# A clock per half of the TensorE array in the scheduler of a fused attention and feed-forward kernel

## Chip, cores and metric

The kernel runs on one core of a Trainium2 chip. The metric is the device time of one execution in microseconds (us); the time that counts is the median of several executions. Profiles come from one further execution each.

## What is computed

`x` is 2048 x 512. A gate per row mixes an attention with 32 query heads, head size 16 and a single shared key and value head, and a feed-forward layer with SiLU:

```python
q = (x @ wq).reshape(B, S, 32, 16).transpose(0, 2, 1, 3)
k, v = x @ wk, x @ wv                          # 2048 x 16 each, shared by all heads
p = softmax(einsum("bhqd,bkd->bhqk", q, k) * 16 ** -0.5)
a = einsum("bhqk,bkd->bhqd", p, v).transpose(0, 2, 1, 3).reshape(B, S, 512) @ wo
b = silu(x @ w1) @ w2                          # w1: 512 x 1792, w2: 1792 x 512
g = sigmoid((x * gate_w).sum(-1, keepdims=True))
out = g * a + (1 - g) * b
```

The exponentials are 32 x 2048 x 2048 values, and they set the size of the problem: ScalarE takes them in 1024 instructions of 128 x 1024.

## The kernel before

**The work.** The attention is cut into 32 rounds: 4 chunks of 512 queries, 4 groups of 8 heads, 2 halves of a group. A round has 16 steps, one for each 128 keys, so there are 512 steps. A step has two parts; each part is one group of eight score products (`scores`, line 1174) into a two-bank PSUM tile `S` and one exponential (line 1180, ScalarE) from `S` to `P`. Then P V sums the step into `pv` (`sums`, line 1278). This is done in one of two ways. A *native* step multiplies the float32 `P` with `VF`. A *split* step takes the upper 16 bits of `P` as they lie (unit "U") and the rest `L` (unit "L"), which VectorE makes with one 128 x 2048 instruction (`low`, line 1199), and multiplies both with `VP`. A native step costs TensorE more, a split step costs VectorE one long instruction.

**The array.** All these products have few rows and columns, so TensorE is used as eight tiles of 64 rows x 32 columns: a lower half (partitions 0 to 63) and an upper half, with four column tiles each. A group of eight score products fills all eight tiles once; so do the eight products of a unit. `pv0` is summed on the lower half, `pv1` on the upper.

**The stream.** Beside the attention runs a stream of 512-column products, given out by the generator `outs()`: hidden blocks of the feed-forward layer (`ffn_h`, 12 products), its outputs (`ffn_o`, 12 or 6), later projections of queries (`q_block`, 12) and of the attention's results (`out_proj`, 12 or fewer). Each such output contracts over 128 rows: its products on the lower 64 rows and those on the upper 64 rows go into one PSUM bank `pm`. Before the change two outputs run in lockstep (`f_slot`, line 835 is the product): while output `cur` does its upper rows, the next output `new` does its lower rows, eight products at a time. When `cur` is done it is evicted (`leave`): by ScalarE's tanh (line 849) and VectorE (line 854), or by VectorE into `acc` (lines 807 and 809), and a new turn starts only when that eviction is over (`f_ready`).

**The order.** Nothing is scheduled by hand: `attention` runs a planner while the program is built. It keeps estimated clocks for TensorE (`pe`), ScalarE (`act`), VectorE (`dve`) and GpSimd (`pool`), a list of VectorE tasks with due times (`put`, `serve`), and in the loop `while p < n_s` decides what TensorE issues next: `sums`, `f_slot`, or the next `scores`, which may not come before the exponential two parts earlier has freed its `S`. The constants in capitals at the file's head are the planner's prices and thresholds: `SLOT` is one group, `PB` the number of `P` buffers, `HURRY` the number of steps behind from which P V goes first. Every engine takes its instructions in the order in which the planner emitted them; waits are semaphores.

**The end.** A round ends with `norm_a`: VectorE transposes `pv0` and `pv1` out of PSUM (lines 1103 and 1104), then GpSimd (in the last round VectorE) adds, rebuilds and normalizes; `turned` makes the 16-bit pairs `O` (lines 1135 and 1136) that `out_proj` needs. After the last scores, `attention` finishes the sums, then the outputs that still run, then all outputs that are left as whole 128-row products (`whole`, line 839), each evicted into `acc` and written out.

The rule that lets a turn of the stream start:

```python
if T_.evicted in tasks:
    return False
if max(T_.free, ahead[0].free if ahead else 0.0) > pe[0]:
    return False
```

## Time and profile before

| what | value |
|---|---|
| time, median of 3 (lowest, highest) | 1075.16 us (1074.93, 1075.76) |
| time of the profiled execution | 1073.23 us |
| its span, first to last instruction | 1071.4 us |
| granted TensorE clock, mean | 0.995 |
| busy: PE, ACT, DVE, POOL | 1023.1, 999.7, 916.6, 471.2 us |
| first exponential starts | 39.3 us |
| split steps (instructions of line 1199) | 245 |

How to read it: PE is TensorE, ACT ScalarE, DVE VectorE, POOL GpSimd. A row of a timeline has the start, the time until the last of the grouped instructions ends, engine, line, operation, out<-in, shape, count, and in brackets how long the engine sat idle before, and for whom. The recorded duration of a matmul holds its way through the array, so consecutive groups overlap in the records; what a group costs is the distance from its start to the next group's start. The clock column is the share of full speed that was granted to TensorE.

### The profile page before, as it was taken

How to read it: one execution, taken by the hardware profiler on the slowest of the kernel's cores; microseconds unless marked ns; L12 is line 12 of the kernel's file. 1: busy time of each engine (PE TensorE's matmuls, PEld its weight loads, DVE VectorE, ACT ScalarE, POOL GpSimd, SP SyncE). 2: the span in 40 equal slices, each digit the busy share in tenths (PEclk: the TensorE clock that was granted, in tenths of full speed). 3: DMA queues.
4: the chain of work that ended last, by engine and by line, in shares of the span. 5: the costliest groups of instructions: out<-in, count | busy, mean ns of one | idle time of the engine just before them, and what ended most of it. 6: DMA issues, size and time to landing. Idle time of an engine off the chain costs nothing.

```text
span 1071.4 us, 65086 instructions
## 1 busy us (share of the span) xinstructions
PE 1023.1 (95%) x30610; PEld 564.2 (53%) x30610; DVE 916.6 (86%) x838; ACT 999.7 (93%) x1121; POOL 471.2 (44%) x388
## 2 busy tenths in 40 slices
PE   8999999999999999999999999999999999999996
PEld 5465454455555545455555555555555555555452
DVE  6799989999999998788797878888889898889784
ACT  5799999999999999999999999999999999999980
POOL 1034345324352373634744335465475267374620
PEclk9999999999999999999999999999999999999998
DMA  5421211100000100000000010000000010000001
GB/s 199 135 61 49 70 41 54 51 12 22 8 18 31 31 22 11 12 19 16 12 22 11 12 60 12 19 7 22 12 11 11 12 47 8 12 11 12 4 5 42
DMA packets 23079, 32.90 MB, mean 31 GB/s; under 512 B 5137, under 2 KB 13074, under 8 KB 22802
## 3 DMA queue, kind: packets, MB, share of 16 engines
q1 hardware_dynamic: 22050, 27.54, 8.4%
q8 instruction: 241, 3.95, 1.6%
q0 software_dynamic: 320, 1.05, 0.3%
q14 instruction: 36, 0.29, 0.1%
q10 hardware_dynamic: 432, 0.07, 0.0%
HBM read 20.12 MB, written 8.52 MB: 27 GB/s over the span
## 4 chain that ended last, share of the span: by engine, by line
PE 38%; ACT 35%; DVE 13%; issue 8%; POOL 4%; DMA 1%; ACTq 0%; SPq 0%; DVEq 0%; POOLq 0%
ACT P L1180 33%; PE pm L835 13%; PE pv L1278 12%; PE S L1174 9%; DVE L L1199 7%; PE pm L839 2%; ACT e L849 2%; POOL T L1109 1%; POOL U L1111 1%; DVE e L854 1%; PE pt L316 1%; DVE acc L809 1%; POOL T L1112 1%; POOL H L856 0%; POOL U L1116 0%
## 5 line engine op out<-in xcount | busy, mean ns | idle before, releaser
L1180 ACT ACTIVATE P<-S 128x1024 f32<-128x1024 f32 x1024 | 959.6, 1079 | 24.4 <-PE S L1174 22.7
L1199 DVE TENSOR_TENSOR L<-P 128x2048 f16<-128x2048 f32 x245 | 606.8, 2491 | 35.8 <-ACT P L1180 35.2
L1174 PE MATMUL S<-qb,KT 50*32 50x512 f16 x8192 | 435.0, 380 | 13.5 <-ACT P L1180 11.0
L1174 PEld LDWEIGHTS <-KT 50*32 50x32 f16 x8192 | 191.6, 89 | 244.5 <-issue 161.1
L1278 PE MATMUL pv<-P,VF 64*32 64x512 f32 (+1 forms) x5360 | 298.2, 503 | 0.0
L835 PE MATMUL pm<-xs,w1s 64*32 64x512 f16 x5376 | 263.7, 375 | 2.3 <-DVE e L854 1.1
L835 PE MATMUL pm<-w2s,H 64*32 64x512 f16 x4896 | 249.2, 375 | 4.9 <-DVE acc L807 2.0
L1109 POOL TENSOR_TENSOR T<-T,U 128x512 f32<-128x512 f32 x31 | 83.8, 2704 | 275.4 <-DVE U L1104 275.4
L856 POOL CAST H<-e 128x512 f16<-128x512 f32 x56 | 57.7, 1030 | 205.9 <-DVE e L854 204.3
L835 PEld LDWEIGHTS <-w1s 64*32 64x32 f16 x5376 | 116.1, 92 | 53.3 <-issue 14.9
L835 PEld LDWEIGHTS <-H 64*32 64x32 f16 x4896 | 106.2, 92 | 46.5 <-issue 6.3
L1278 PEld LDWEIGHTS pv<-P,VF 64*32 64x32 f32 x5360 | 104.7, 106 | 37.4 <-issue 6.6
L857 POOL TENSOR_TENSOR H<-e,H 128x512 f16<-128x512 f32 x56 | 108.8, 1943 | 4.5
L1278 PE MATMUL pv<-P,VP 64*32 64x512 bf16 x1952 | 108.1, 388 | 1.2 <-DVE U L1104 0.6
L1278 PE MATMUL pv<-L,VP 64*32 64x512 f16 x1952 | 103.3, 375 | 3.1 <-DVE L L1199 2.8
L1278 PEld LDWEIGHTS <-VP 64*32 64x32 f16 x3904 | 67.8, 93 | 45.1 <-issue 20.9
L835 PE MATMUL pm<-xs,wqs 64*32 64x512 f16 x1152 | 83.9, 375 | 1.1 <-DVE e L854 1.0
L854 DVE SCALAR_TENSOR_TENSOR e<-e,pm 128x512 f32<-128x512 f32 x56 | 38.3, 683 | 43.2 <-ACT e L849 42.9
L835 PE MATMUL pm<-wo_s,O 64*32 64x512 f16 x1440 | 68.3, 382 | 3.2 <-DVE acc L809 1.8
L1116 POOL TENSOR_TENSOR U<-U 128x48 f32<-128x48 f32 (+1 forms) x62 | 57.4, 925 | 2.4
L809 DVE SCALAR_TENSOR_TENSOR acc<-pm,g,acc 128x512 f32<-128x512 f32 x48 | 35.7, 744 | 14.6 <-PE pm L839 8.0
L1111 POOL TENSOR_TENSOR U<-T,mu 128x96 f32<-128x96 f32 x31 | 45.5, 1468 | 2.4
(175 smaller groups left out, 623.6 us busy)
## 6 DMA issues: line engine op xcount, KB each, us to landing
qb<-qd SPq DMA_DIRECT2D x192, 32.0 KB
raw<-in_B_w_dram SPq DMA_DIRECT2D x22, 256.0 KB
xn<-in_A_x_dram SPq DMA_DIRECT2D x8, 512.0 KB
out_dram<-acc SPq DMA_DIRECT2D x16, 256.0 KB
qd<-qx SPq DMA_DIRECT2D x12, 256.0 KB
raw<-in_B_w_dram POOLq DMA_DIRECT2D x4, 256.0 KB, 3.1
raw<-in_A_wo_dram SPq DMA_DIRECT2D x4, 256.0 KB
qb<-sh SPq DMA_DIRECT2D x62, 2.0 KB
```

The lines of the kernel that those rows point to most:

```text
L809: nc.vector.scalar_tensor_tensor(a, po, gate[:, n:n + 1], a, op0=OP.mult, op1=OP.add)
L835: nc.tensor.matmul(self.bank[32 * m:32 * m + 32], l(i, rows, 32 * m), r(j, rows), start=first, stop=last)
L854: nc.vector.scalar_tensor_tensor(e, e, 1.0, ph, op0=OP.add, op1=OP.mult)
L856: nc.gpsimd.tensor_copy(H[:, 0], e)
L857: nc.gpsimd.tensor_tensor(H[:, 1], e, H[:, 0], op=OP.subtract)
L1109: eng.tensor_tensor(T, T, U, op=OP.add)
L1111: eng.tensor_tensor(z[:, :, 1:1 + DIGITS], T3[:, :, 17:17 + DIGITS], mu[:, :, 1:].to_broadcast([128, 16, DIGITS]), op=OP.mult)
L1116: eng.tensor_tensor(first, first, second, op=OP.add)
L1174: nc.tensor.matmul(sc[32 * m:32 * m + 32, f], KT[b:b + 50, k0:k0 + 32], qtile[i][b:b + 50, j], start=True, stop=True)
L1180: nc.scalar.activation(P[:, 2 * j:2 * j + 2], sc, AF.Exp, scale=scale_of(c, o))
L1199: nc.vector.tensor_tensor(L[s], P, upper(P), op=OP.subtract)
L1278: nc.tensor.matmul(pvs[i][h][32 * j:32 * j + 32, cols], a[r], b[r, j, cols], start=start, stop=rest == n)
```

## The change

The planner gets a clock for each half of the array, `half[0]` and `half[1]`, and `pe` only follows them.

- `sums(s, h)` emits the four products of one half; which steps are done, opened and closed is kept for each half, and the two halves of a step need not be neighbours. `norm_a` gets one PSUM task per half (one transpose each).
- The stream no longer runs in lockstep. Two banks `pm0` and `pm1` replace the pool of two; an output starts on whichever half is free, and its second part runs on the other half, once a later score group has waited for a semaphore that covers its first part (`synced`, `marks`) and `GUARD` has passed. `f_slot` emits four products of one output.
- `choose(h, ...)` decides for the half whose clock is behind; if it finds nothing, the other half is asked, then the next scores come.
- `low` of odd steps is made only if a step is at least `SPARE` = 1 ahead (before 0); `HURRY` goes from 4 to 5, so the stream goes ahead of P V for longer.
- After the last scores the remaining outputs run on both halves, and whole products are taken as soon as a bank is free, without first emptying VectorE's task list; the last attention outputs wait for their planned time instead of going first.

The core of the diff:

```diff
-SLOT, VSLOT, LOW, V_PART, BLOCK, ONE_LATE = 0.2165, 0.23, 2.37, 1.7, 3.65, 0.3
-LATER, HURRY, PIECE, PB, FIRST_LOW, LASTB, NEAR, FRESH, SPARE = 0.2, 4, 5.6, 5, 6, 4, 4, 8, 0
+SLOT, VSLOT, LOW, V_PART, BLOCK, ONE_LATE, GUARD = 0.2165, 0.23, 2.37, 1.7, 3.65, 0.2, 0.2
+LATER, HURRY, PIECE, PB, FIRST_LOW, LASTB, NEAR, FRESH, SPARE = 0.2, 5, 5.6, 5, 6, 4, 4, 8, 1
...
-        def issue(n, dur):
-            if sent[0] // 256 != (sent[0] + n) // 256:
-                pe[0] = crossed[0] = max(pe[0], crossed[0] + BLOCK)
-            sent[0] += n
-            pe[0] += dur
+        def issue(h, n, dur):
+            start = max(half[h], floor[0])
+            if sent[0] // 256 != (sent[0] + n) // 256:
+                start = crossed[0] = floor[0] = max(start, crossed[0] + BLOCK)
+            sent[0] += n
+            half[h] = pe[0] = start + dur
...
-        def f_slot():
-            i, cur, new = T_.i, T_.cur, T_.new
+        def f_slot(o, h):
             for m in range(4):
-                if new and i < new.n:
-                    new.product(i, lo, m, i == 0, False)
-                if cur and i >= T_.n - cur.n:
-                    cur.product(i - T_.n + cur.n, hi_, m, False, i == T_.n - 1)
-            issue(16, SLOT)
+                o.product(o.i, (lo, hi_)[h], m, o.i == 0 and not o.second, o.second and o.i == o.n - 1)
+            issue(h, 8, SLOT)
...
             for j in range(4):
-                for h, r in enumerate((lo, hi_)):
-                    nc.tensor.matmul(pvs[i][h][32 * j:32 * j + 32, cols], a[r], b[r, j, cols], start=start, stop=rest == n)
+                nc.tensor.matmul(pvs[i, h][32 * j:32 * j + 32, cols], a[r], b[r, j, cols], start=start, stop=rest == n)
...
+        def choose(h, now, room, behind):
+            n = sums_next(h, now, room, behind >= HURRY)
+            o = f_here(h, now) if room >= SLOT else None
+            if n is not None and last_of(n, h, room) and behind < LASTB and (not o or o.n - o.i < FRESH):
+                n = None
+            if n is not None and (behind >= HURRY or not o):
+                return lambda: sums(n, h, room)
+            if o:
+                return lambda: f_slot(o, h)
...
-                    urgent.extend((c, 0 if late else end, lambda t=t: out_proj(c, all_, t)) for t in range(4))
+                    urgent.extend((c, end, lambda t=t: out_proj(c, all_, t)) for t in range(4))
...
         while True:
-            while tasks:
-                do(min(tasks, key=lambda t: t[0]))
-            o = ahead.pop() if ahead else fetch()
-            if o is None:
+            now = pe[0] = max(half)
+            serve(now)
+            b = bank(now)
+            o = fetch(b) if b and not ended[0] else None
+            if o:
+                for n in range(o.n):
+                    o.whole(n, n == 0, n == o.n - 1)
+                    both(SLOT)
+                leave(o)
+            elif ended[0] and not tasks:
                 break
-            for n in range(o.n):
-                o.whole(n, n == 0, n == o.n - 1)
-            force(o.evict(o.bank))
+            else:
+                both(0.05)
```

What this moves is seen best at two places of the built programs. The first is TensorE's order at a native step right after a group of scores; the two names `pv_...` before are the sums of the lower and the upper half. Before:

```order
L1174 MATMUL S<-qb_81,KT 32x512
L1278 MATMUL pv_14627<-P,VF 32x512
L1278 MATMUL pv_14628<-P,VF 32x512
L1278 MATMUL pv_14627<-P,VF 32x512
L1278 MATMUL pv_14628<-P,VF 32x512
```

and at such a place now, where `pm_2837` is an output of the stream:

```order
L1174 MATMUL S<-qb_81,KT 32x512
L1290 MATMUL pv_2803<-P,VF 32x512 x4
L840 LDWEIGHTS wqs
L840 MATMUL pm_2837<-xs,wqs 32x512
L840 LDWEIGHTS wqs
L840 MATMUL pm_2837<-xs,wqs 32x512
```

The eight products of a native step alternated between the halves; now four products of one half stand together, and the other half's stream stands behind them.

The second place is VectorE's order from the last round's sums (line 1116 ends them) to the last output. `pm` is an output's bank; `g_65` marks an output of the feed-forward layer, `gg` one of the attention. Before:

```order
L1116 TENSOR_TENSOR T<-T,U 128x16
L809 SCALAR_TENSOR_TENSOR acc<-pm,g_65,acc 128x512
L1124 RECIPROCAL rr<-T 128x16
L1127 TENSOR_TENSOR C<-T,rr 128x16x16
L1133 STREAM_TRANSPOSE T<-C 128x512
L1135 CAST O<-T 128x512
L1136 TENSOR_TENSOR O<-T,O 128x512
L809 SCALAR_TENSOR_TENSOR acc<-pm,gg,acc 128x512 x4
L809 SCALAR_TENSOR_TENSOR acc<-pm,g_65,acc 128x512 x7
```

and now, up to the first of the four attention outputs:

```order
L814 SCALAR_TENSOR_TENSOR acc<-pm_32988,g_65,acc 128x512
L814 SCALAR_TENSOR_TENSOR acc<-pm_33021,g_65,acc 128x512
L1124 RECIPROCAL rr<-T 128x16
L1127 TENSOR_TENSOR C<-T,rr 128x16x16
L814 SCALAR_TENSOR_TENSOR acc<-pm_33392,g_65,acc 128x512
L1133 STREAM_TRANSPOSE T<-C 128x512
L1135 CAST O<-T 128x512
L1136 TENSOR_TENSOR O<-T,O 128x512
L814 SCALAR_TENSOR_TENSOR acc<-pm_33402,g_65,acc 128x512
L814 SCALAR_TENSOR_TENSOR acc<-pm_33415,g_65,acc 128x512
L814 SCALAR_TENSOR_TENSOR acc<-pm_33423,g_65,acc 128x512
L814 SCALAR_TENSOR_TENSOR acc<-pm_33431,gg,acc 128x512
```

After the last round's sums stood one eviction, the four attention outputs and seven feed-forward outputs; now there are six feed-forward outputs, three of them inside the normalization, and the four attention outputs come last.

Counted over the built programs, in the attention and its end:

| count | before | now |
|---|---|---|
| split steps, native steps | 244, 268 | 235, 277 |
| stream products on half tiles (w1s, w2s, wqs, wo_s) | 5376, 4896, 1152, 1440 | 5376, 5184, 1152, 1440 |
| whole w2s products and whole wo_s products after the last scores | 60, 12 | 24, 12 |
| TensorE instructions of P V that wait for VectorE | 274 | 227 |
| TensorE instructions of the stream that wait for VectorE | 141 | 136 |

359 lines of the change are left out of this document (191 added, 168 removed).

## The prediction

> **What bounds the kernel now.** I read the page's groups first, then the exponential's own line, then timelines of single engines, last the windows with the clock.
>
> ```profile
> PE 1023.1 (95%) x30610; PEld 564.2 (53%) x30610; DVE 916.6 (86%) x838; ACT 999.7 (93%) x1121; POOL 471.2 (44%) x388
> L1199 DVE TENSOR_TENSOR L<-P 128x2048 f16<-128x2048 f32 x245 | 606.8, 2491 | 35.8 <-ACT P L1180 35.2
> ```
> ```profile
> L1180 ACT ACTIVATE P<-S x1024: 1015/1068/1278, 39.3 to 1037.6; 128x1024 f32<-128x1024 f32 x171
>   PE S L1174: 22.7, 42
> ```
> ```profile
> 247.13 45.26 ACT L1180 ACTIVATE P<-S 128x1024 f32<-128x1024 f32 x49
> 292.21 0.67 ACT L849 ACTIVATE e<-pm 128x512 f32<-128x512 f32 x1
> 292.69 5.69 ACT L1180 ACTIVATE P<-S 128x1024 f32<-128x1024 f32 x6
> 1033.10 5.72 ACT L1180 ACTIVATE P<-S 128x1024 f32<-128x1024 f32 x6
> ```
>
> All exponentials lie between 39.3 and E = 1033.10 + 5.72 = 1038.8 us, a stretch of 999.5 us. Undisturbed, 49 of them go from start to start of the next instruction in 292.21 - 247.13 = 45.08 us, 0.920 each, and a tanh costs 0.48. So ScalarE needs 1024 x 0.920 + 55 x 0.48 = 968.5 us of the 999.5. It waits 22.7 us for scores, in 42 places; the remaining 8 us are the first exponentials and small change. **ScalarE bounds the stretch; what a scheduler can win in it is at most about 22.7 us.** Ahead of 39.3 us nothing of weight changes. Behind E lie 1071.4 - 1038.8 = 32.6 us, in which no exponential runs: the tail.
>
> TensorE's load is worked out from prices, since its busy time counts a matmul's whole way through the array:
>
> ```profile
> 1008.04 1.28 PE L835 MATMUL pm<-wo_s,O 64*32 64x512 f16 x40
> 1009.12 0.41 PE L1174 MATMUL S<-qb,KT 50*32 50x512 f16 x8
> ```
> ```profile
> 1017.13 1.04 PE L1278 MATMUL pv<-P,VF 64*32 64x512 f32 x16
> 1017.99 0.40 PE L1174 MATMUL S<-qb,KT 50*32 50x512 f16 x8
> ```
> ```profile
> 1029.94 0.43 PE L1278 MATMUL pv<-P,VP 64*32 64x512 bf16 x8
> 1030.17 0.42 PE L1278 MATMUL pv<-L,VP 64*32 64x512 f16 x8
> ```
>
> Forty stream products, five groups of eight, take 1009.12 - 1008.04 = 1.08 us, 0.2165 a group; a native step 0.86; a unit U or L 0.23. With the counts of the order: scores 1024 x 0.2165 = 222, stream 12,864 / 8 x 0.2165 = 348, units 488 x 0.23 = 112, native 268 x 0.86 = 230, together 912 us, some of it behind E. So TensorE has about 9% to spare on the mean, and the 22.7 us come from places where its work stands unevenly. Two kinds are seen:
>
> ```profile
> 580.48 20.47 ACT L1180 ACTIVATE P<-S 128x1024 f32<-128x1024 f32 x22 [0.54 <-PE S L1174]
> ```
> ```profile
> 1013.37 0.63 PE L835 MATMUL pm<-wo_s,O 64*32 64x512 f16 x8 [1.35 <-DVE acc L809]
> ```
> ```profile
> 1014.49 1.02 ACT L1180 ACTIVATE P<-S 128x1024 f32<-128x1024 f32 x1 [1.11 <-PE S L1174]
> 1016.20 1.02 ACT L1180 ACTIVATE P<-S 128x1024 f32<-128x1024 f32 x1 [0.68 <-PE S L1174]
> ```
> ```profile
> 1013.00:1014.00 1.00, 0.63 (x16) 0.34 (x23) 1.00 (x3) 0.38 (x1) 0.00 (x0) 0.62 0.00 0
> 1014.00:1016.00 2.00, 2.00 (x48) 0.90 (x40) 2.00 (x2) 1.02 (x1) 1.39 (x1) 0.50 0.03 8
> 1016.00:1018.00 2.00, 2.00 (x57) 0.76 (x49) 0.71 (x1) 1.63 (x2) 1.92 (x2) 0.84 0.00 0
> ```
>
> The first is a native step in front of scores that were already due: about half a microsecond, some twenty times. The second is TensorE held by an eviction: 1.35 us of waiting, and then the granted clock falls to 0.50 for about three microseconds, so one such wait cost ScalarE 1.8 us.
>
> **Do the halves run apart?** The change rests on that, and the trace before answers it. In the order, three groups of line 835 (twelve products, all on the lower half) stand ahead of one group of scores and one U and one L unit, each of which alternates between the halves. The records:
>
> ```profile
> 314.55 0.40 PE L835 MATMUL pm<-wo_s,O 64*32 64x512 f16 x4 [0.48 <-DVE acc L809]
> 314.60 0.41 PE L1174 MATMUL S<-qb,KT 50*32 50x512 f16 x4
> 314.76 0.40 PE L835 MATMUL pm<-wo_s,O 64*32 64x512 f16 x4
> 314.82 0.41 PE L1278 MATMUL pv<-P,VP 64*32 64x512 bf16 x4
> 314.98 0.40 PE L835 MATMUL pm<-wo_s,O 64*32 64x512 f16 x4
> 315.06 0.40 PE L1278 MATMUL pv<-L,VP 64*32 64x512 f16 x4
> 315.19 0.40 PE L1174 MATMUL S<-qb,KT 50*32 50x512 f16 x4
> ```
>
> Four of the eight scores start at 314.60, and four of U and four of L follow, while the lower half is still at its second and third group; the lower half's four scores come at 315.19, 0.59 us behind. So a half overtakes the other by at least 0.59 us past the program's order, and a busy half does not stop the free one. The Trainium skill says otherwise ("TensorE: Matmul & The Clock Gate", Part 3, "The mechanism"): there matmuls start and end strictly in program order, only weight loads are pulled ahead. By that rule scores would bind both halves together; what this would give is the second rival below, and the rows above speak against it.
>
> **The change part by part.**
>
> *The tail.* Before:
>
> ```profile
> 1040.42 0.72 DVE L1103 STREAM_TRANSPOSE T<-pv 128x512 f32<-128x512 f32 x1
> 1041.06 0.68 DVE L1104 STREAM_TRANSPOSE U<-pv 128x512 f32<-128x512 f32 x1
> 1044.20 0.74 DVE L809 SCALAR_TENSOR_TENSOR acc<-pm,g,acc 128x512 f32<-128x512 f32 x1
> 1044.86 0.24 DVE L1124 RECIPROCAL rr<-T 128x16 f32<-128x16 f32 x1
> 1045.60 0.71 DVE L1133 STREAM_TRANSPOSE T<-C 128x512 f32<-128x512 f32 x1
> 1046.81 0.69 DVE L1136 TENSOR_TENSOR O<-T,O 128x512 f16<-128x512 f32 x1
> 1064.72 0.75 DVE L809 SCALAR_TENSOR_TENSOR acc<-pm,g,acc 128x512 f32<-128x512 f32 x1 [0.54 <-PE pm L839]
> ```
> ```profile
> 1046.83 4.63 PE L839 MATMUL pm<-wo_s,O 128*128 128x512 f16 x12 [3.54 <-DVE O L1135]
> 1051.57 13.11 PE L839 MATMUL pm<-w2s,H 128*128 128x512 f16 x60
> ```
> ```profile
> 1047.00:1050.00 3.00, 2.88 (x8) 0.89 (x7) 1.77 (x3) 0.00 (x0) 0.00 (x0) 0.56 0.00 0
> ```
>
> TensorE idles 3.54 us for the normalization, does twelve products at a clock of 0.56, and only then sixty w2s products, 13.1 us. The last eviction ends at E + 26.6, the writes 5.9 us later. Now only 24 whole w2s products are left, they lie beside the normalization, and the attention's come last. Step by step from E: behind the last scores (they end at about E - 1.5, since the last exponential starts at 1037.6) the upper half has 0.86 + 3 x 0.2165 + 2 x 0.23 + 0.86, and then 2 x 0.23 + 0.86: it ends at E + 2.6, its transpose at E + 3.5 (before E + 2.9). The sums take 1044.20 - 1041.74 = 2.5 us, to E + 6.0; two evictions (1.5), the reciprocal and C (0.7) to 8.2; the first whole output (bank free at E + 6.7, six products 1.3, 0.2 on the way) is evicted to 9.0; the rest of the normalization, 1.9, to E + 10.9. Seven evictions are left, 0.75 us each, and the fourth to seventh wait now and then for a bank and three products (0.65): the last ends at E + 17.1. With the writes, 5.9, that is E + 23. TensorE idles some 2 us on the way, so the clock may fall as above: six products then take 2.6 instead of 1.3. I add 1 us: E + 24 instead of E + 32.6, **-8.6 us** (bounds -9.6 with a full clock, -6 with a low clock twice and crowded writes).
>
> *The stretch up to E.* It takes in 36 groups more of the stream (288 w2s products, 7.8 us) and nine native steps for split ones, 9 x (0.86 - 0.46) = 3.6 us: 11.4 us more TensorE work, covered by its spare 9%; if that cover failed, it would cost 11.4. VectorE has ten long instructions fewer (10 x 2.49 = 25 us), so evictions meet them less often. One tanh more lies ahead of E: **+0.5 us**. What the halves gain shows in the work between two score groups: by the order's counts and the prices above, before 47 of the 1023 stretches hold more than 1.1 us for a half, now 38, and taken as the mean of both halves 29; pairs of stretches with a mean over 0.75 fall from 35% to 24%. The native kind of wait should lose half or more of its places. The evictions are as many, with nearly as many waits (141 before, 136 now), but an output need no longer wait for its neighbour's eviction while the other bank is free. So of 22.7 us I take back **-10 us** (between nothing and -18; nearest to the change in long stretches).
>
> *Added waits.* The second part of an output waits for a score group and `GUARD`; behind it on TensorE stands nothing that is not already planned later, and the other bank fills the time. Banks, DMAs and their queues are as before: nothing.
>
> Sum: 1073.2 - 8.6 - 10 + 0.5 = 1055.1 for a profiled execution. The median of the runs lies 1075.16 - 1073.23 = 1.9 above, so **1057 us**.
>
> **The rivals.**
> 1. *Only the tail gains.* The 22.7 us stay because the waits come from durations the planner does not know, such as the eviction at 1013. For it: both kinds were planned around before, too. 1073.2 - 8.6 + 0.5 + 1.9 = 1067 us.
> 2. *The halves bind at the scores.* Then the longer half counts in every stretch: by the same counts the sum of the longer halves goes from 695 to 791 us, with the scores 917 and 1012 us. Above ScalarE's 968 TensorE would bound, 1012 + 10 to 25 of waits for 999.5: +22 to +37, with the tail 1089 to 1104. The rows at 314.55 speak against it. This is where the page named above would lead.
> 3. *Starved queue, slower than before.* A semaphore wait holds TensorE's queue for both halves. If the tighter packing lets it run into evictions like that at 1013, each costs ScalarE 1.8 us as there, the fallen clock included. It decides from five such waits more, which undo the tail (5 x 1.8 = 9); with ten, 1075.2 - 8.1 + 18 = 1085 us. For it: the stream now has priority (`HURRY` 5) and ends its outputs in pairs; against: 47 waits of P V fewer.
>
> **How the numbers follow.** Forecast 0.55, only the tail 0.24, bound halves 0.06, starved queue 0.15. About 0.2% can be told from no change here, 1073.0 to 1077.3. The first two are faster; the third and most of the fourth are slower, and a milder fourth ends within the band: faster 0.79, same 0.06, slower 0.15. The range goes from 1047, where all but 5 us of the waits and 9.6 of the tail are won, to 1074, beyond rival 1 and a mild rival 3; what lies above is about 0.18.
>
> **What would show it.** Right: ScalarE's wait for scores about 12 us, the last exponential near 1030, the tail about 24 us with 24 whole w2s products ahead of O. Wrong: the wait above 23 us, low clock in windows before E, or records in which the four scores of a free half wait for the busy one.

## The result, and the profile after

The changed kernel takes **1076.78 us** (median of 12 runs, 1075.69 to 1080.51) against 1074.79 us of the kernel before in the same comparison (12 runs, 1072.5 to 1075.9): ratio **1.0026, 95% interval 1.0014 to 1.0038**, slower by a quarter of a per cent. Forecast were 1057 us and faster. The profiled execution took 1076.07 us, its span is 1074.3.

The page and the exponential's own line, after:

```profile
PE 1036.9 (97%) x31150; PEld 668.5 (62%) x31150; DVE 881.0 (82%) x828; ACT 1005.1 (94%) x1121; POOL 454.1 (42%) x388
```
```profile
L1184 ACT ACTIVATE P<-S x1024: 1014/1045/1182, 39.6 to 1050.3; 128x1024 f32<-128x1024 f32 x171
  PE S L1174: 27.3, 36
```

The last exponential now starts at 1050.3 (before 1037.6) and ends at E = 1051.35 (before 1038.8). ScalarE's waits for scores did not halve, they rose from 22.7 to 27.3 us, in fewer places. So the stretch of exponentials **lost 12.4 us** (first start to last start 998.3, now 1010.7), and the tail **won 9.7** (32.6, now 22.9). The tail's VectorE, after:

```profile
1053.25 0.72 DVE L1103 STREAM_TRANSPOSE T<-pv 128x512 f32<-128x512 f32 x1 [1.40 <-PE pv L1290]
...
1059.54 0.75 DVE L814 SCALAR_TENSOR_TENSOR acc<-pm,g,acc 128x512 f32<-128x512 f32 x1 [0.82 <-PE pm L844]
1060.21 0.70 DVE L1133 STREAM_TRANSPOSE T<-C 128x512 f32<-128x512 f32 x1
...
1061.40 0.69 DVE L1136 TENSOR_TENSOR O<-T,O 128x512 f16<-128x512 f32 x1
...
1067.87 0.75 DVE L814 SCALAR_TENSOR_TENSOR acc<-pm,gg,acc 128x512 f32<-128x512 f32 x1 [0.24 <-PE pm L844]
```

The transposes begin at E + 1.9, the first whole output is evicted by E + 8.9, `O` is ready at E + 10.7, the last eviction ends at E + 17.3, and the span 5.7 us later.

What of the stretch? I took the distance from each of ScalarE's instructions to the next and subtracted the undisturbed pace of these traces (0.918 behind an exponential, 0.476 behind a tanh). What is left over, by size (count, us; the last two columns are experiments told below):

| gap | before | after | e10_bound | e15_bound_06 |
|---|---|---|---|---|
| 0.06 to 0.3 us | 79, 11.6 | 132, 18.1 | 128, 17.1 | 126, 16.5 |
| 0.3 to 1 us | 40, 22.5 | 27, 13.8 | 19, 10.1 | 20, 11.8 |
| over 1 us | 5, 6.5 | 12, 18.4 | 5, 9.4 | 5, 6.8 |

The middle class, in which the native steps in front of due scores lie, fell by 8.7 us as the change meant it; part of it only became smaller, since the class below grew by 6.5. Over all kernels told below but the two with less load, e3_slack and e9_level, the two classes together hold 34.1 to 36.5 us with pairs of halves and 25.8 to 32.3 us with a clock per half. So the halves do shorten the short gaps, by some 6 us on the mean (about 2 of these go to intervals that lie under 0.06 us above the pace and stand in no class). In the changed kernel **seven long gaps more, 11.9 us, outweigh that.** TensorE's waits between 39 and 1040 us (line, what for, us in total, times, longest), before and then after:

```profile
PE S L1174 <- ACT P L1180: 11.0, 30, 1.0
PE pm L835 <- DVE e L854: 5.1, 7, 1.0
PE pm L378 <- DVE e L944: 3.3, 5, 1.2
...
PE pv L1278 <- DVE U L1104: 0.6, 3, 0.2
PE pv L1278 <- DVE T L1103: 0.5, 1, 0.5
```
```profile
PE pv L1290 <- DVE T L1103: 8.5, 10, 1.6
PE pm L378 <- DVE e L949: 6.0, 4, 2.2
...
PE pv L1290 <- DVE U L1103: 1.4, 3, 0.7
...
PE pm L840 <- DVE e L859: 0.9, 3, 0.5
PE S L1174 <- ACT P L1184: 0.3, 1, 0.3
```

Before, TensorE stood 11 us in front of scores whose bank ScalarE had not yet freed: it had a lead. After, 0.3: no lead. The stream's own waits for evictions (line 835, with those for `acc` 9.8 us in 13 places) are nearly gone (line 840, 0.9), which the prediction had hoped for. But two kinds of waits for VectorE stand out now: a round's first P V behind the transposes, 9.9 us for 1.1, and line 378, 6.0 for 3.3. Line 378 is the bound of a query block: two small matmuls that read `e`, the magnitudes which VectorE makes last of all in that block's eviction. One of them, VectorE, TensorE and ScalarE in turn:

```profile
193.28 0.74 DVE L814 SCALAR_TENSOR_TENSOR acc<-pm,g,acc 128x512 f32<-128x512 f32 x1
193.93 0.68 DVE L934 TENSOR_SCALAR qx<-pm 128x512 f16<-128x512 f32 x1
194.65 0.69 DVE L935 SCALAR_TENSOR_TENSOR qx<-pm,qx 128x512 f16<-128x512 f32 x1
195.26 0.28 DVE L949 TENSOR_SCALAR e<-qx 128x512 uint16<-128x512 uint16 x1
```
```profile
195.59 0.39 PE L378 MATMUL pm<-e,kab 64*32 64x512 f16 x2 [2.21 <-DVE e L949]
195.60 0.60 PE L1174 MATMUL S<-qb,KT 50*32 50x512 f16 x8
```
```profile
196.29 2.17 ACT L1184 ACTIVATE P<-S 128x1024 f32<-128x1024 f32 x2 [2.20 <-PE S L1174]
```

The two matmuls came into TensorE's queue while VectorE was still at the eviction in front of the query's; the scores behind them waited 2.21 us, on both halves, and ScalarE 2.20. Such are four of the twelve long gaps (196.3, 253.7, 313.6, 384.5; 6.5 us together), three lie behind late transposes (274.6, 495.0, 842.9; 4.3), and one of 2.6 at 799.5 looks like the stall of the last section. The kernel before waits at line 378 too: the gaps of ScalarE that follow four of its five waits come to 3.5 us, so against that kernel the bounds account for 3 us more, not for 6.5. The granted clock is 1.00 in every window from 25 to 1050 us; no fallen clock has a part in this.

### The profile page after: what moved, and what is told of

It is laid out like the page before. It is cut to its first block, busy times and chain, and to the rows that moved or that the text cites. A ratio compares the mean times of both kernels' runs of the same rounds, so it can differ in the third digit from the quotient of the medians.

```text
span 1074.3 us, 66167 instructions
## 1 busy us (share of the span) xinstructions
PE 1036.9 (97%) x31150; PEld 668.5 (62%) x31150; DVE 881.0 (82%) x828; ACT 1005.1 (94%) x1121; POOL 454.1 (42%) x388
## 5 line engine op out<-in xcount | busy, mean ns | idle before, releaser
L1184 ACT ACTIVATE P<-S 128x1024 f32<-128x1024 f32 x1024 | 962.5, 1055 | 30.1 <-PE S L1174 27.3
L1203 DVE TENSOR_TENSOR L<-P 128x2048 f16<-128x2048 f32 x235 | 570.7, 2440 | 67.7 <-ACT P L1184 63.9
L1174 PE MATMUL S<-qb,KT 50*32 50x512 f16 x8192 | 539.7, 380 | 0.8 <-ACT P L1184 0.3
L1290 PE MATMUL pv<-P,VF 64*32 64x512 f32 (+1 forms) x5792 | 496.7, 489 | 0.6 <-issue 0.6
L840 PE MATMUL pm<-w2s,H 64*32 64x512 f16 x5184 | 314.5, 375 | 0.4 <-DVE acc L814 0.3
L840 PE MATMUL pm<-xs,w1s 64*32 64x512 f16 x5376 | 313.8, 375 | 0.8 <-DVE e L859 0.7
L1290 PEld LDWEIGHTS pv<-P,VF 64*32 64x32 f32 x5792 | 183.3, 106 | 33.1 <-issue 3.4
L1290 PE MATMUL pv<-P,VP 64*32 64x512 bf16 x1880 | 177.8, 387 | 11.0 <-DVE T L1103 8.5
L1290 PE MATMUL pv<-L,VP 64*32 64x512 f16 x1880 | 169.1, 375 | 1.9 <-DVE L L1203 1.4
L840 PEld LDWEIGHTS <-H 64*32 64x32 f16 x5184 | 143.6, 92 | 40.8 <-issue 6.1
L1290 PEld LDWEIGHTS <-VP 64*32 64x32 f16 x3760 | 103.0, 92 | 47.1 <-issue 24.2
```

Source lines behind the costliest of these rows:

```text
L840: nc.tensor.matmul(self.bank[32 * m:32 * m + 32], l(i, rows, 32 * m), r(j, rows), start=first, stop=last)
L1174: nc.tensor.matmul(sc[32 * m:32 * m + 32, f], KT[b:b + 50, k0:k0 + 32], qtile[i][b:b + 50, j], start=True, stop=True)
L1184: nc.scalar.activation(P[:, 2 * j:2 * j + 2], sc, AF.Exp, scale=scale_of(c, o))
L1203: nc.vector.tensor_tensor(L[s], P, upper(P), op=OP.subtract)
L1290: nc.tensor.matmul(pvs[i, h][32 * j:32 * j + 32, cols], a[r], b[r, j, cols], start=start, stop=rest == n)
```

## The experiments

All ratios are to the kernel before, run on the same chip.

| kernel | median us | ratio, 95% interval | E | tail | wait for e |
|---|---|---|---|---|---|
| e1_tail | 1069.12 | 0.9956, 0.994 to 0.9972 | 1039.6 | 27.3 | 3.3 |
| e2_joint | 1078.54 | 1.0042, 1.0025 to 1.0059 | 1047.9 | 28.7 | 7.7 |
| e3_slack | 1108.69 | 1.0317, 1.0299 to 1.0335 | 1042.2 | 65.2 | 9.1 |
| e4_before_tight | 1066.72 | 0.9943, 0.9924 to 0.9962 | 1043.4 | 20.9 | 0.8 |
| e6_merge | 1073.13 | 0.9989, 0.9978 to 1.0 | 1049.6 | 23.7 | 6.0 |
| e7_mild_tail | 1069.37 | 0.9952, 0.9936 to 0.9968 | 1045.1 | 23.8 | 0.9 |
| e8_const_tail | 1068.74 | 0.9943, 0.9922 to 0.9964 | 1044.2 | 22.4 | 1.2 |
| e9_level | 1091.22 | 1.0153, 1.0127 to 1.018 | 1045.5 | 43.9 | 3.9 |
| e10_bound | 1064.47 | 0.9907, 0.9888 to 0.9927 | 1037.6 | 25.6 | none |
| e11_close | 1069.25 | 0.9953, 0.9939 to 0.9968 | 1045.5 | 23.7 | 6.3 |
| e12_both | 1068.01 | 0.9946, 0.9927 to 0.9965 | 1045.2 | 20.9 | none |
| e13_low | 1078.04 | 1.0028, 1.001 to 1.0045 | 1050.6 | 22.9 | 6.8 |
| e14_low_bound | 1067.35 | 0.9923, 0.9894 to 0.9951 | 1046.0 | 20.4 | none |
| e15_bound_06 | 1058.48 | 0.9834, 0.9804 to 0.9863 | 1037.1 | 20.2 | none |
| e16_pairs | 1071.10 | 0.9956, 0.994 to 0.9972 | 1043.1 | 27.5 | 1.0 |
| e17_third | 1070.45 | 0.996, 0.9944 to 0.9975 | 1046.9 | 22.8 | 7.2 |
| e18_third_bound | 1061.76 | 0.9884, 0.9861 to 0.9907 | 1040.0 | 19.8 | 0.4 |

E is the end of the last exponential, the tail what follows of the span, the last column line 378's wait for `e` in the stretch, all in us. E, the tail and the waits are from one profiled execution of each kernel. The first exponential starts at 39.1 to 40.4 us, in e17 at 41.5, so where kernels are compared closely below, the stretch from there to E is taken. Three executions of one and the same order of the stretch (before, e1, e5) have 999.5, 999.7 and 999.1 us.

**First round: is the tail worth what was worked out, and which part costs the stretch?** The theory was a *tight plan*: the scheduler's own clock, printed while the program is built, sets the last exponential 971.6 us behind the first before and 971.4 after, and the chip falls behind it by 26.7 and 39.2 us (the *slip*); with the halves it places scores with less slack. The rival was the closing of rounds by halves.

e1_tail, on the kernel before (`flight` holds the evictions that are not over):

```diff
-                end = on_pool(2.8, dve[0])
+                end = dve[0] + 1.3 if late else on_pool(2.8, dve[0])
...
-                    urgent.extend((c, 0 if late else end, lambda t=t: out_proj(c, all_, t)) for t in range(4))
+                    urgent.extend((c, end, lambda t=t: out_proj(c, all_, t)) for t in range(4))
...
-            while tasks:
-                do(min(tasks, key=lambda t: t[0]))
+            serve(pe[0])
+            flight = [f for f in flight if f[0] in tasks or f[1] > pe[0]]
+            o = None
+            if len(flight) < 2:
+                o = ahead.pop() if ahead else next(seq, 0)
```

> The kernel before with the reordered tail alone: the attention's products wait for the normalization and the 60 whole w2s products come ahead of them, each output evicted when a bank is free. The stretch of exponentials is instruction for instruction that of before, so every theory puts the last exponential at 1038.8 us (within 1). The tail, 32.6 us before: sixteen evictions of 0.75 us and about 7 us of normalization on VectorE from about E + 2.9, and 5.9 us of writes: E + 27, so 1069 us (1066 to 1072). If the tail's gain in the changed kernel came from having 24 instead of 60 whole products and not from their order, the tail stays near E + 32 and the time near 1074.

1069.12 us, the tail 27.3 us, both as expected. After the last exponential TensorE now has work beside the normalization:

```profile
1044.03 5.35 PE L839 MATMUL pm<-w2s,H 128*128 128x512 f16 x24
1049.22 0.81 PE L839 MATMUL pm<-wo_s,O 128*128 128x512 f16 x3
...
1052.54 7.93 PE L839 MATMUL pm<-w2s,H 128*128 128x512 f16 x36
```

The tail alone is a gain of half a per cent, and it lies in the order of the end.

e2_joint, on the changed kernel:

```diff
-                nc.vector.transpose(T if h == 0 else U, pv)
-                closed[i, h] = dve[0] + 0.06
+                nc.vector.transpose(T, halves_pv[i][0])
+                nc.vector.transpose(U, halves_pv[i][1])
+                closed[i, 0] = closed[i, 1] = dve[0] + 0.06
```

> The changed kernel, but both halves' sums of a round leave PSUM in one task, as before (the two transposes follow each other, and neither half may open its next round earlier). The scheduler's own clock puts the last exponential 971.4 us behind the first in the changed kernel and 973.5 in this one; the chip took 39.2 us more than that in the changed kernel (26.7 in the kernel before). Theory of the round boundaries (a half's first P V of a round waits in TensorE's queue for a transpose that VectorE does late, and holds both halves): the slip against the scheduler's clock falls to 33 or less, and the waits of pv for T and U fall below 12 us. Theory of the tight plan (scores are placed with less slack ahead of the exponential, so many small delays reach ScalarE): the slip stays at 37 to 41. Total time: 72 whole products in the tail for 24, so 8 us more there; 1074 to 1079 by the first, 1084 to 1089 by the second.

The slip fell to 33.8, between the two theories, and the waits of pv to 6.9 us, yet E only by 3.4, and 48 whole products more went to the tail. It decided nothing at the time; seen from the end, its order had its own early bounds (7.7 us).

e3_slack, on the changed kernel, and e4_before_tight, on the kernel before, change LATER alone:

```diff
-LATER, HURRY, PIECE, PB, FIRST_LOW, LASTB, NEAR, FRESH, SPARE = 0.2, 5, 5.6, 5, 6, 4, 4, 8, 1
+LATER, HURRY, PIECE, PB, FIRST_LOW, LASTB, NEAR, FRESH, SPARE = 0.1, 5, 5.6, 5, 6, 4, 4, 8, 1
```
```diff
-LATER, HURRY, PIECE, PB, FIRST_LOW, LASTB, NEAR, FRESH, SPARE = 0.2, 4, 5.6, 5, 6, 4, 4, 8, 0
+LATER, HURRY, PIECE, PB, FIRST_LOW, LASTB, NEAR, FRESH, SPARE = 0.3, 4, 5.6, 5, 6, 4, 4, 8, 0
```

> The changed kernel with LATER 0.1 for 0.2: TensorE may be given work until 0.1 us (not 0.2) behind the moment at which a bank for the next scores comes free. The scheduler's slack between the end of scores and their exponential rises from 0.155 us on the mean to 0.237 (before: 0.193), the places with less than 0.1 us fall from 520 to 318 (before: 359); its own stretch falls from 971.4 to 959.5 us, since fewer tanh and fewer late scores lie in it; and 192 whole products more are left for the tail, 192 x 0.2165 = 41.6 us. Theory of the tight plan: the slip against the scheduler's clock falls from 39.2 to 22-30 us, so the last exponential ends near 1051 - 12 - 13 = 1026 (1022 to 1031), the time is about 1092. Theories of the round boundaries or of halves that hold each other: the slip stays at 36 or more, the last exponential near 1038, the time about 1104.

> The kernel before (pairs of halves in one step, one clock) with LATER 0.3 for 0.2: slack on the mean 0.145 us for 0.193, places with less than 0.1 us 538 for 359, much as in the changed kernel, but no half has a clock of its own and every round closes as before. The scheduler's own stretch is 983.0 us for 971.6, and no whole w2s product is left for the tail (60 before: 13 us less there). Theory of the tight plan: the slip rises from 26.7 to 35-42 us, the last exponential ends near 1038.8 + 11.4 + 11 = 1061, the time is about 1081. Theories that blame the halves' clocks or the closing of rounds by halves: the slip stays at 25 to 30, the last exponential ends near 1050, the time is about 1070.

**As the reason for the slip the tight plan fell on both sides.** With more slack the slip did not fall to 22 to 30, it was 41.3; with less slack on the kernel before it did not rise to 35 to 42, it fell to 20.3. The small gaps did go with the slack, 7.6 us in e3_slack for 18.1 and 13.9 in e4_before_tight for 11.6; but e3_slack has less load as well, and its order had 9.1 us of waits at line 378. And e4_before_tight, with no whole w2s product left for the tail, was faster than both kernels. 13 us of work moved ahead of E cost 4.6 there, and 3.0 of that is a one-off stall (last section).

**Second round: the order in TensorE's queue.** e5_bench, one execution, adds TensorE work behind the end of the kernel before, in ten patterns (`one` is a matmul, `lock` alternates the halves, `runs` puts k groups on one half and then k on the other):

```diff
+            def lock(n, f=one):
+                for _ in range(n):
+                    for m in range(4):
+                        for h in range(2):
+                            f(h, m)
...
+            lock(32)
+            for k in (1, 2, 4, 8):
+                nc.tensor.drain()
+                runs(32, k)
```

> The kernel before with TensorE work alone added behind its end, in ten patterns with a drain ahead of each. A group is four matmuls on one half (scores' shape, 0.2165 us); each of the first five patterns holds 32 groups a half: (1) halves alternating matmul by matmul, as before's stream; then runs of (2) 1, (3) 2, (4) 4 and (5) 8 groups on one half and then as many on the other; (6) 32 groups on the lower half alone; (7) eight native steps of P V, halves alternating matmul by matmul; (8) the same by halves, four and four; (9) eight times a native step on the lower half and then 4 groups on the upper; (10) eight times the same work with one matmul of the native step ahead of each group. Halves that run apart without bound: all of 1 to 10 take 6.9 us. Queue theory (one queue starts the matmuls in order, and a half can be fed past the other only by about 0.59 us, 2.7 groups, as the rows at 314.55 showed): 1 to 4 take 6.9, (5) 9 us, (9) 6.9. If the look-ahead is less than one group, 2 to 5 take 10 to 13.9. Theory of the weight loads (loads on one half in a row do not overlap, those on alternating halves do): (2) takes 7.3 or more, (1) 6.9, (8) as (7).

From the starts of the records, first to last of each pattern (31 groups later: 6.7 us; the sixth and seventh ran at a fallen clock, last section):

```
alternating 6.72 | runs of 1: 6.72 | of 2: 7.04 | of 4: 7.34 | of 8: 8.31
native by halves (4 and 4) 6.51 | native, then 4 groups on the other half 6.92 | interleaved 6.74
```

Four in a row on one half cost nothing against alternating ones, so the theory of the weight loads fell. Runs of two and four groups cost 5 and 9%, where the queue theory had nothing, and runs of eight less than its 9 us. In the runs of eight, the first 0.92 us hold 16 matmuls, one half alone, and the next 0.88 us 36, both halves:

```profile
1094.20:1095.12 0.92, 0.85 (x16) 0.45 (x20) 0.00 (x0) 0.00 (x0) 0.00 (x0) 1.00 0.00 0
1095.12:1096.00 0.88, 0.88 (x36) 0.51 (x32) 0.00 (x0) 0.00 (x0) 0.00 (x0) 1.00 0.07 19
```

The upper half starts when four of the lower half's eight groups have started, as from one queue in which a half is fed past the other by four groups, 0.87 us. The Trainium skill ("TensorE: Matmul & The Clock Gate", Part 3, "The mechanism") has matmuls start strictly in program order; here too the trace differs.

e6_merge writes the changed kernel's matmuls between two score groups in the order of their planned starts, so that overlapping groups of the halves alternate:

```diff
+        def flush():
+            for _, _, f in sorted(held, key=lambda e: e[:2]):
+                f()
+            held.clear()
...
-            for m in range(4):
-                o.product(o.i, (lo, hi_)[h], m, o.i == 0 and not o.second, o.second and o.i == o.n - 1)
+            hold(h, SLOT, [lambda m=m: o.product(*a, m, *e) for m in range(4)])
```

> The changed kernel with the same plan, but the matmuls between two groups of scores are written into the program in the order of their planned starts, matmul by matmul: where groups of the two halves overlap in time, they alternate as in the kernel before, instead of four and four. If the order of weight loads or of matmuls in TensorE's queue (four in a row on one half) is what costs the changed kernel its 12.4 us in the stretch, at least half comes back: last exponential at 1045 or earlier, time 1066 to 1071. If the stretch is lengthened by what the plan lets stand between scores (closings of rounds, more TensorE work) the last exponential stays at 1049 to 1053, time 1074 to 1079.

E 1049.6, 1.8 us earlier, inside the range that speaks against the order as the reason (the time, 1073.1, is 0.9 below its range). e7_mild_tail is e1_tail with LATER 0.25:

> The candidate that takes the two parts that gained: the kernel before with the reordered tail and LATER 0.25 (36 whole products in the tail for 60). Last exponential between before's 1039 and the 1043.4 of LATER 0.3: 1041. Tail 27.3 - 24 x 0.2165 = 22.1: 1041 + 22.1 + 2.3 for what lies around the span = 1065 us (1063 to 1068), as fast as or faster than all kernels so far. No theory of the halves speaks on it; should the last exponential come at 1045 or later, a plan with less slack does cost after all.

E came at 1045.1, not 1041, 5.4 us behind e1_tail for 24 whole products (5.2 us) that left the tail; 3.2 us of it are a one-off stall (last section). The time was that of e1_tail, above its range.

**Third round: load, or halves?** e8_const_tail is e1_tail with the changed kernel's constants, e9_level the changed kernel with level clocks at each group of scores:

```diff
-SLOT, VSLOT, LOW, V_PART, BLOCK, ONE_LATE = 0.2165, 0.23, 2.37, 1.7, 3.65, 0.3
-LATER, HURRY, PIECE, PB, FIRST_LOW, LASTB, NEAR, FRESH, SPARE = 0.2, 4, 5.6, 5, 6, 4, 4, 8, 0
+SLOT, VSLOT, LOW, V_PART, BLOCK, ONE_LATE = 0.2165, 0.23, 2.37, 1.7, 3.65, 0.2
+LATER, HURRY, PIECE, PB, FIRST_LOW, LASTB, NEAR, FRESH, SPARE = 0.2, 5, 5.6, 5, 6, 4, 4, 8, 1
```
```diff
             sc = pS.tile([128, 2, 512], F32, name="S")
+            half[:] = 2 * [max(half)]
```

> The kernel before with the reordered tail and the changed kernel's three constants (ONE_LATE 0.2, HURRY 5, SPARE 1), but with pairs of halves and one clock. It has as many whole w2s products in the tail as the changed kernel (24), and TensorE's load up to the last exponential is 918.2 us (before 909.7, changed 921.2; mean of the halves, scores included). It differs from the changed kernel in the halves alone. Theory of the load (the stream's priority puts 11.5 us more TensorE work in front of the last exponential, and that is what costs): last exponential at 1049 to 1052, time 1073 to 1076. Theory of the halves (the load costs about 4 us, as with LATER 0.25 and 0.3 on the kernel before, the halves' own clocks the other 8): last exponential at 1041 to 1046, time 1065 to 1070.

> The changed kernel, but the scheduler brings both halves' clocks to the later one ahead of each group of scores, so that it no longer counts on a half that runs ahead past the scores; halves differ only between two groups of scores. It places less: TensorE's load up to the last exponential is 894.1 us (changed 921.2), the sum of the longer halves with the scores 940 (changed 1012, before 917), and 144 whole products are left for the tail (24). The kernels with halves so far lie on one line of last exponential against load: 1042.2 at 880.5, 1047.9 at 911.3, 1051.4 at 921.2; by it 1044.5 is expected here. Theory that halves hold each other at the scores (what one half does beyond the other between two groups of scores delays the scores, and is never won back): the last exponential comes well below the line, at 1034 to 1040. Theory that they don't: on the line, 1043 to 1046. The tail has 120 whole products more, 26 us: time 1084 to 1090 by the first, 1093 to 1097 by the second.

e8: E 1044.2, as the theory of the halves had it. By the stretches from the first exponential on (999.5 before, 1004.3 here, 1011.8 after), **4.8 us come with the load and the constants, 7.5 with the halves**, from one order each. And 3.4 of the 4.8 are again a one-off stall, which e16 below has too, at 2.9 us, without e8's constants; so it is not shown to come from the load. e9: E 1045.5, on the line, so halves that hold each other at the scores are not the reason; its tail was 5 us shorter than worked out, and its time lies between the two ranges.

**Fourth round: the early bounds.** What else do the halves change? Each bank has its own free time now. The rule that lets a bound go, before and after:

```diff
-            return bounds and not T_.going and T_.cur and not ahead and T_.evicted not in tasks and T_.free <= pe[0]
+            return bounds and bank(min(half)) is not None
```

Neither asks for the operand `e`. Before, `T_.free` was set by the end of the last eviction, and that is the query's own, which ends with `e`: the bank's rule covered the operand by the way. After, the other bank may be free sooner. On the scheduler's own clock no bound stands ahead of its operand before; after, four do, by 1.1 to 1.6 us, in the very places where the chip waits 6.0. (The five shorter waits of the kernel before are not on that list: there the operand came late on the chip although the plan had it in time.)

e10_bound (and, with other constants, e14, e15 and e18) asks for the operand; e11_close opens a round later; e12_both does both:

```diff
                 bounds.append((o, c, qa))
+                asked[0] = dve[0] + 0.4
...
-            return bounds and bank(min(half)) is not None
+            return bounds and asked[0] <= min(half) and bank(min(half)) is not None
```
```diff
-                closed[i, h] = dve[0] + 0.06
+                closed[i, h] = dve[0] + 0.3
```

> The changed kernel, but a query bound (the two matmuls of line 378, which read the tile e that VectorE writes last) is put into TensorE's order only 0.4 us after the scheduler's VectorE has ended the task that writes it; in the changed kernel a free bank alone was enough. Load 920.6 us (921.2), 36 whole products in the tail (24). Queue theory (a matmul that waits for VectorE holds both halves, and TensorE has no lead to lose any more): the waits of line 378 for e, 6.0 us in four places of the stretch, fall below 1.5; ScalarE's four long gaps behind them (196.3, 253.7, 313.6, 384.5 us, together 6.5) go, and the last exponential, 1051.4, comes at 1044 to 1047; time 1071 to 1074. Theory of the capacity (TensorE is full, what one wait gives back the next takes): last exponential at 1049 to 1053, time 1075 to 1079.

> The changed kernel, but a half's next round may be opened only 0.3 us (not 0.06) after the scheduler's clock has the transpose of its sums done, so that a late VectorE does not stop TensorE's queue. Load 920.8 us (921.2), 24 whole products in the tail, as in the changed kernel. Queue theory: the waits of pv for T and U, 9.9 us, fall to 6 or less, and with them go some 3 us of ScalarE's gaps (495.0, 274.6 and 842.9 were 4.3 together): last exponential at 1047 to 1049.5, time 1072 to 1075. Theory of the capacity: last exponential at 1050 to 1053, time 1076 to 1079.

> Both edits, the bound put off until its operand is due and 0.3 us of margin at the closing of rounds. Load 923.5 us (changed 921.2, pairs with the same constants 918.2), 24 whole products in the tail. Queue theory: the gains add, last exponential at 1041 to 1045, near the 1044.2 of the pairs with the same constants; time 1066 to 1070: the halves' clocks cost nothing any more once their order has no early waits. Theory of the capacity, or that the halves hold each other: last exponential at 1048 to 1053, time 1073 to 1079.

e10: TensorE's waits and ScalarE's line:

```profile
PE pv L1291 <- DVE U L1104: 2.4, 4, 1.0
PE pv L1291 <- DVE T L1104: 2.3, 3, 0.9
```
```profile
L1185 ACT ACTIVATE P<-S x1024: 1012/1045/1228, 39.8 to 1036.6; 128x1024 f32<-128x1024 f32 x171
...
  PE S L1175: 17.1, 24
```

No wait of line 378 for `e` is left, ScalarE waits 17.1 us for 27.3, E = 1037.6: 13.7 us earlier for 6.0 us of waits, more than the theory had said. P V's waits for transposes fell too, to 4.7 from 9.9, and its edit doesn't touch them. e11 took 5.8 (waits of pv 4.5 for 9.9), again more than it should. e12 did not add them: E 1045.2, its time inside the range only by a shorter tail. So each edit also deals a new order of the whole program, and an order is worth some us either way. The last round tests whether the early bounds are the cause or such luck: the same pair on other orders (e13 and e14 with LOW 2.40 for 2.37, e17 and e18 with 2.44), a larger delay (e15), and the rule on the pairs of e1_tail (e16).

```diff
-SLOT, VSLOT, LOW, V_PART, BLOCK, ONE_LATE, GUARD = 0.2165, 0.23, 2.37, 1.7, 3.65, 0.2, 0.2
+SLOT, VSLOT, LOW, V_PART, BLOCK, ONE_LATE, GUARD = 0.2165, 0.23, 2.4, 1.7, 3.65, 0.2, 0.2
```
```diff
-                asked[0] = dve[0] + 0.4
+                asked[0] = dve[0] + 0.6
```
```diff
-            return bounds and not T_.going and T_.cur and not ahead and T_.evicted not in tasks and T_.free <= pe[0]
+            return bounds and asked[0] <= pe[0] and not T_.going and T_.cur and not ahead and T_.evicted not in tasks and T_.free <= pe[0]
```

> A second plan of the changed kernel, as a control: LOW 2.40 for 2.37, which shifts the scheduler's VectorE clock a little and reorders much; nothing else. Load 923.4 us, 24 whole products in the tail. On the scheduler's own clock four query bounds stand ahead of their operand again (1.1 to 1.6 us), as in the changed kernel. Queue theory: line 378 waits for e some 5 us, last exponential at 1047 to 1053, time 1072 to 1079. If the 13.7 us of the put-off bound were only the luck of another order, this order may lie anywhere between 1037 and 1053.

> The control's LOW 2.40 with the bound put off until 0.4 us after its operand. Load 924.9 us, 18 whole products in the tail. Queue theory: line 378 waits less than 1.5 us, and the last exponential comes at least 4 us ahead of the control's. Luck theory: within 3 us of the control's, or behind it.

> The changed kernel with the bound put off until 0.6 us (not 0.4) after its operand: a third order without early bounds. Load 923.4 us, 24 whole products in the tail. Queue theory: last exponential at 1037 to 1046, time 1062 to 1070. Luck theory: anywhere up to 1053.

> The kernel before with the reordered tail and the same rule for the bound (0.4 us after its operand). In the kernel before no bound stands ahead of its operand on the scheduler's clock (a bank was free only when the query's own eviction had ended), so the rule should change little: last exponential at 1036 to 1041 (1039.6 without it), time 1066 to 1070. If the rule wins 5 us or more here too, it is not the halves' two banks that made the early bounds cost.

> A third plan of the changed kernel: LOW 2.44 for 2.37, nothing else. Load 923.2 us, 24 whole products in the tail; four query bounds stand 1.4 to 1.5 us ahead of their operand on the scheduler's clock. Three pairs of orders with and without early bounds gave the last exponential 13.7, 4.6 and 0.3 us earlier without them, 6.2 on the mean, for about 6 us of waits: queue theory puts this order, with early bounds, at 1045 to 1053, time 1070 to 1078. If the three pairs were luck, it may lie below 1045 as well.

> LOW 2.44 with the bound put off until 0.4 us after its operand. Load 927.2 us, 6 whole products in the tail. Queue theory: the last exponential 2 to 12 us ahead of the other kernel with LOW 2.44, 1036 to 1046; with a tail of about 20 us the time is 1058 to 1068. Luck theory: as likely behind it as ahead.

Line 378's waits in e13, e17 and e18, and e15's exponentials:

```profile
PE pm L378 <- DVE e L949: 6.8, 4, 2.2
```
```profile
PE pm L378 <- DVE e L949: 7.2, 4, 2.0
```
```profile
PE pm L378 <- DVE e L949: 0.4, 1, 0.4
```
```profile
L1185 ACT ACTIVATE P<-S x1024: 1014/1042/1222, 39.9 to 1036.0; 128x1024 f32<-128x1024 f32 x171
...
  PE S L1175: 13.7, 23
```

Four pairs of orders, with early bounds and without: E 1051.4 to 1037.6, 1045.5 to 1045.2, 1050.6 to 1046.0, 1046.9 to 1040.0. From the first exponential on (e17's starts 2.2 us behind e18's) the pairs differ by 14.0, 0.4, 5.0 and 4.8 us, **6.0 on the mean for 6.0 to 7.2 us of waits**. The spread shows how much an order adds. The second pair shows no difference: e11's profiled execution was the longest of its nine, and by the medians less the tails e12 is even 1.6 us behind. All kernels with a clock per half at a load of 920 to 927 us together: the stretch is 1005.5 to 1011.8 us in the five with early bounds (after, e6, e11, e13, e17) and 997.2 to 1005.9 in the five without (e10, e12, e14, e15, e18), 7 us apart on the mean. e17 lay inside its range, e18 as well. On the pairs the rule won nothing (e16: E 1043.1, 3.4 later than e1 and 2 behind its range, a stall of 2.9 us included; the time is 1.1 above its range). e15's E lay at the lower end of its range, its time 3.5 below, the tail being shorter. **e15 beats both kernels: 1058.48 us, 0.9834 (0.9804 to 0.9863)**, the changed kernel with the bound's rule mended; it is the best of five such orders, whose medians go from 1058 to 1068.

## Why the prediction was wrong

- *ScalarE bounds the stretch, 22.7 us to win at most*: right as a limit. ScalarE's pace is unchanged; only its waits moved.
- *TensorE has about 9% to spare, which covers 11.4 us more work*: too generous. Against ScalarE's 968 us the load of 910 leaves 6%. e8 has about the changed kernel's load (918 us for 921) without the halves, and its E is 5.4 us later than before's; e4's is 4.6 later for 13 us of work, e7's 5.4 later than e1's for 5. Between 3.0 and 3.4 us of each are a one-off stall whose cause is open; about 2 us are left as the cost of the load.
- *The halves run apart*: right, by up to 0.87 us (e5), and no run showed them held at the scores (e9; the second rival fell).
- *The tail, -8.6*: right, and the best term: E + 22.9 against E + 23 with a full clock (E + 24 taken); single steps came within 0.6 us of their forecasts.
- ***The stretch, -10*: this step failed**, at +12.4. Its reason held in part: the middle class of gaps lost 8.7 us, 6.5 came back as small gaps, and the stream's waits for evictions nearly went. What failed stood in the next paragraph, *Added waits*: "Banks, DMAs and their queues are as before: nothing". The banks were not as before. Two banks with a free time each let a bound into the queue ahead of its operand; I read the rule for a turn of the stream, not the one for a bound. TensorE's waits at line 378 went from 3.3 to 6.0 us, and orders without early bounds are 6.0 us shorter on the mean of four pairs. The other added wait, a round's first P V behind the transposes, went from 1.1 to 9.9 us; what it costs was not separated.
- *`GUARD`*: right to cost nothing. With 0.3 the very same program is built.
- *The third rival, a starved queue, at 0.15*: this is what came. It priced a wait at 1.8 us, with five more undoing the tail; there were seven gaps over 1 us more, 11.9 us, 1.7 each. That the price fits is luck: the 1.8 held a fallen clock, which had no part in the changed kernel, and one of the gaps, 2.6, looks like the one-off stall. The place was wrong, too (bounds and first P V, not evictions). I had counted against it that P V has 47 waits fewer; the number of waits said nothing here, since their length grew.
- *The range from 1047*: its own terms, with the half microsecond of the tanh, give 1048. Nothing hangs on it.

The sum as it came, by the profiled executions: tail -9.7; first exponential 0.3 later; stretch +12.3; together +2.9, as the spans differ (the medians differ by 2.0). The 12.3 are 4.8 of load and constants (e8, the stall included) and 7.5 of the halves. Of the 7.5, early bounds are about 6 by the four pairs, measured against orders that wait for no bound; the kernel before does wait for some, and against it ScalarE's gaps give 3. The split rests on one order for each part and is good to some us only. What stays open is the rest of the halves' gain. The five orders without early bounds have E at 1037 to 1046, three of pairs at a like load (e4, e7, e8) at 1043 to 1045; that is 3 us on the mean, within what an order is worth, so a gain of the halves in the whole stretch is not shown, although the two short classes of gaps are smaller in every order with halves. The waits at the opening of rounds (9.9 us after) were only touched together with other things.

## What to carry to other kernels

Where a planner keeps several engines' order, ask of each rule that is loosened what else it guaranteed by the way: here a bank's free time had stood for an operand that nobody asked for. Here two small matmuls that waited 2.21 us were paid for by the scores behind them and by ScalarE (2.20 us), so compare the planner's own time of each operand with the time at which its reader is placed; that list needs no chip and named the four places, though not the shorter waits of the kernel before. And when an edit reorders a whole program, one run of it is one draw: repeat the pair on a second and third order before believing its size.

## What the runs showed of the hardware

**The clock fell while one half worked without a pause.** e5's sixth pattern keeps the lower half alone busy from 1103.04 us on; windows (the seventh number column is the granted clock):

```profile
1103.00:1105.00 2.00, 1.96 (x39) 1.00 (x43) 0.00 (x0) 0.00 (x0) 0.00 (x0) 1.00 0.04 8
1106.00:1114.00 8.00, 8.00 (x80) 3.20 (x76) 0.00 (x0) 0.00 (x0) 0.00 (x0) 0.50 0.00 0
1114.00:1118.00 4.00, 3.92 (x40) 0.91 (x40) 0.00 (x0) 0.00 (x0) 0.00 (x0) 0.50 0.02 4
1120.00:1122.00 2.00, 2.00 (x48) 0.54 (x35) 0.00 (x0) 0.00 (x0) 0.00 (x0) 1.00 0.00 0
```

It went to 0.50 some two to three us after the start and came back only when both halves had worked for 4 us. The Trainium skill ("TensorE: Matmul & The Clock Gate", Part 1, "What's actually happening") ties the low clock to an idle window of about 3.4 us; TensorE was not idle here. One run shows it, and no wait of the changed kernel's stretch hangs on it. Nor did a wait decide by its length alone: in the kernel before the clock fell behind one of 1.35 us (at 1013), in the changed kernel it stayed at 1.00 behind one of 2.21 (window 194 to 196). In some of the other orders the clock fell inside the stretch, in e10 to 0.51 from 891 to 894 us, ahead of a gap of 2.6 at 895.2; that is part of what an order adds.

**A one-off stall.** In most orders TensorE and ScalarE stop together once between 750 and 805 us, for nothing that the profile names; in e8:

```profile
769.51 1.14 PE L835 MATMUL pm<-xs,w1s 64*32 64x512 f16 x21 [2.90 <-issue]
```
```profile
770.11 1.02 ACT L1180 ACTIVATE P<-S 128x1024 f32<-128x1024 f32 x1 [3.24 <-remote]
```

ScalarE's gap there is 3.0 us in e4, 3.2 in e7, 3.4 in e8, 3.9 in e9, 4.0 in e12, 3.5 in e14 and 2.9 in e16, and no gap between 750 and 805 us is over 1.1 in the kernel before and e1; the changed kernel's longest, 2.6 us at 799.5, lies there too. e16 differs from e1 in the bound's rule alone, so more load is not needed for it. In these microseconds TensorE gets only a few matmuls, some more than 1 us apart, and the profile puts the idle time between them down to issue (1.02 and 1.31 us in e9, 1.00 and 1.21 in e16). Why it comes in some orders was not tried.
